# Three float32r passes for two of the second layer's seven products, with the split of their operands a step ahead

## The chip, the cores and the metric

The kernel runs on one core of one Trainium2 chip. The metric is device time of one execution, in microseconds (us), lower is better; times shown are medians of runs.

## The reference

A Fourier mixing of 8 batches of 3008 x 256 numbers (the real part of a two-dimensional transform over sequence and features) is followed by a two-layer network on the 24064 rows:

```
X = fft(x, axis=1); X = fft(X, axis=2); x = X.real.reshape(24064, 256)
h = x @ w_in                       # 256 -> 2048
g = h * clip(h + 3, 0, 6) / 6      # hard swish
out = g @ w_out                    # 2048 -> 256
```

## The kernel before

The transform is done in three parts. Stage one (`fold`, `stage1`) adds mirrored inputs on GpSimd (POOL) and multiplies them on TensorE (PE) by a cosine and sine table for 47 of the 3008 = 47 x 64 points; its result `z` goes to DRAM and comes back turned as `g`. Stage two (`stage2`) multiplies by the tables of the 64 points and leaves a chunk of 256 columns in one PSUM bank, which is copied into `q`. The transform over the 256 features is folded into `w_in` at the start, so that the first layer takes `q` directly.

The work is cut into four pairs of batches with 12 chunks each, 48 chunks in all, and every chunk into eight steps (`fc`), each for 256 of the 2048 hidden units. The last chunk of each pair has 192 columns in the second layer.

**First layer.** From chunk 3 on its products are exact splits into float32r: `split_q` splits `q` into `KQ` (high, low and rest), `split_w` has done so with the weights (`KW`), and three passes (`passes`, order rest, high, low) replace a float32 product. The work is arranged in units of 512 columns (`Unit`), mostly *joint*: the same weights for two neighbouring chunks. A unit is made up of a seed in PSUM (`seed`, ScalarE, ACT), three even passes, a copy of that sum (`keep_even`, ACT, into `s`), three odd passes into the same bank (`odd_half`), a relu of it (ACT), the value for the mirrored output `v = u - 2 s` (`other_sign`, VectorE, DVE), its relu (ACT), and two gates on DVE that write the hidden values into a slot of `A`.

**Second layer.** A 2 x 2 block product by seven products instead of eight (the weights `G` hold seven blocks, 0 = B11, 1 = B21 and so on). Products 0, 1 and 2 take `A` as it is; products 3 to 6 take sums of its blocks, which POOL makes one step ahead (`combine`, tile `c`). The seven products of a step accumulate over the eight steps in four banks (`acc`), in float32. `close`, `finish`, `store` and `turn` join the seven results at a chunk's end (`e`), transpose them on DVE into `o` and send `o` in eight DMAs of 32 KB for each half.

**Order of the work.** The schedule is written out by hand: each engine runs its instructions in the order in which the program issues them. From step 22 on, one turn of the main loop (a *cycle*) issues the odd half of one unit, the even half of the next and a share of the product stream. `place` says how many products a cycle takes (6 to 8), `due` by when a unit must be gated. `Feed` lets POOL do `fold` work when its estimated backlog allows. PSUM has four banks for `acc`, two for units (`a0`, `a1`) and two others (`y0`, `y1`): `v` lives in `y0`; stage two takes `y1`; stage one takes both. The order within one cycle before the change is: seed of the next unit; odd passes and relu; one product; stage one, where there is a piece; other sign and its relu; one product; even passes and copy `s`; the two gates; transposes; stage two, where there is one; the other products; closing and sums.

Buffers: four `x` tiles, two `z`, two `o`, two `s`, one `q` kept to the end.

Of the kernel before, what the change touches and what calls it, by code (L numbers as in the profile page):

```python
# [60 lines left out]
def kernel(  # L61
# [38 lines left out]
    xpool = ctx.enter_context(tc.tile_pool(name="xpool", bufs=4))  # L100
    ypool = ctx.enter_context(tc.tile_pool(name="ypool", bufs=1))
    zpool = ctx.enter_context(tc.tile_pool(name="zpool", bufs=2))
# [25 lines left out]
    NSLOT, CHUNK1 = 9, 3  # L128
    SPLIT = CHUNK1 * NF - 2
# [12 lines left out]
    G = consts.tile([P, 7, NF, P], F32, name="G")  # L142
# [15 lines left out]
    def x_tile(pool=xpool, tag="x", bufs=None):  # L158
        return pool.tile([P, XC, D], F32, tag=tag, bufs=bufs, name="xt")
# [8 lines left out]
    def load_forward(pr, c):  # L168
        xt = x_tile()
# [14 lines left out]
    def load_partners(pr, c):  # L184
        xr = x_tile()
        pr.xr[c] = xr
        i = pr.p * NXC + c
        gather(xr, IX[:, i:i + 1])
# [14 lines left out]
    def take_half(hb, m, pool=xpool, tag="x"):  # L203
        hb.x[m], hb.xr[m] = x_tile(pool, tag), x_tile(pool, tag)
# [167 lines left out]
    def evict_first(hb, m, ps, pt):  # L372
        k = FIRST.index(m)
        pool, tag = ((zpool, "z"), (zpool, "z"), (wpool, "z"), (wpool, "z"))[k]
        z = pool.tile([P, 2, 2, D + 1], F32, tag=tag, bufs=2, name="z")
# [100 lines left out]
    Q = []  # L476

    def q_tile(pr, gr):
        if pr.p == gr == 0:
            pr.q[0] = early.tile([P, 2, 2 * TB], F32, tag="q", name="q")  # L480
            return
        if not Q:
            Q.append(qpool.tile([P, 2, 2 * TB], F32, tag="q", name="q"))
        pr.q[gr] = Q[0]

    def stage2_half(hb, gr, copy=nc.scalar.copy, ps=None, tab=None):

        vg, i = hb.b * NSG // 2 + gr // 2, gr % 2
        if i == 0:
            q_tile(first, vg)  # L490
# [16 lines left out]
        copy(first.q[vg][:, :, i * TB:(i + 1) * TB], ps)  # L507

    def spread_part(pr, n, cols):

        i = n % 2 * TB
        qd = dpool.tile([1, TB], F32, tag="qd", name="qd")
        nc.sync.dma_start(out=qd[:, 0:cols], in_=pr.q[n // 2][P - 1:P, 1, i:i + cols])
# [13 lines left out]
    def stage2(pr, gr, i, copy=nc.scalar.copy):  # L527

        if i == 0:
            q_tile(pr, gr)  # L530
# [12 lines left out]
        copy(pr.q[gr][:, :, i * TB:i * TB + n], ps[:, :, 0:n])  # L543

# [6 lines left out]
    class Chunk:  # L551
# [3 lines left out]
        def __init__(self, pr, ck):  # L555
# [8 lines left out]
            self.n_all = pr.p * NCK + ck  # L564
            k1 = [(ck * KK + j // 2 + 1) % NK1 for j in range(KC)]
# [28 lines left out]
    def activate(ch, fc, u, v, between=None):  # L594
        nq, qn = ch.nq, QN[:, ch.n_all % 4]
        s = spool.tile([P, 2, TB], F32, tag="s", name="s")
# [6 lines left out]
        pool, tag, bufs = (early, "a", 3) if ch.n_all * NF + fc < SPLIT else (zpool, "z", 2)  # L603
# [14 lines left out]
    def split_q(ch):  # L618

        of, nq, q = ch.ck % 2 * TB, ch.nq, ch.pr.q[ch.ck // 2]  # L620
        high, low, rest = (KQ[:, j, :, ch.n_all % 3, 0:nq] for j in range(3))
        yield from split(high, low, rest, q[:, :, of:of + nq])

    def split(high, low, rest, x):
        nc.scalar.mul(high, x, 1.0 - EPS / 2.0)  # L625
        h = high.bitcast(F32)
        nc.gpsimd.tensor_tensor(low, x, h, op=AL.subtract)  # L627
        yield OPERATION
        nc.scalar.mul(rest, h, EPS)  # L629
        nc.gpsimd.tensor_tensor(rest, rest, low, op=AL.subtract)  # L630
        yield OPERATION
# [74 lines left out]
    def keep_even(un):  # L706
        un.s = spool.tile([P, 2, TB], F32, tag="s", name="s")
        nc.scalar.copy(un.wide(un.s[:]), un.wide(un.u[:]))  # L708
# [20 lines left out]
    def gates(un, m):  # L729

        h, t = (un.u, un.v)[m], un.t[:, m]
        wide = [k for k, (ch, _) in enumerate(un.parts) if not ch.last]
# [43 lines left out]
    def mlp2_first(ch, fc, halves=(0, 1)):  # L776
        a = ch.a[fc]
        for h in halves:
            if fc == 0:
                ch.acc[h] = ps_a.tile([P, 2, TB], F32, tag="acc", name="acc")  # L780
            for f in range(2):
                nc.tensor.matmul(ch.acc[h][:], G[:, (B11, B12, B21, B22)[2 * f + h], fc, :], a[:, :, f],  # L782
# [7 lines left out]

    def mlp2(ch, fc, lo, hi):
# [3 lines left out]
        order = list(enumerate(moving))  # L795
        if ch.final and fc == NF - 1:

            order[5:] = order[:4:-1]
# [4 lines left out]
        for i, mv in order[lo:hi]:  # L803

            if fc == 0 and i % 2 == 0:
                ch.acc[i // 2] = ps_a.tile([P, 2, TB], F32, tag="acc", name="acc")
            nc.tensor.matmul(ch.acc[i // 2][:, i % 2, 0:ch.n], G[:, i, fc, :], mv,  # L807
                             start=(fc == 0 and i % 2 == 0), stop=(fc == NF - 1), skip_group_check=True)
            if fc == NF - 1 and (i % 2 == 1 or i == 6):
                if i == 1:  # L810
                    ch.e = epool.tile([P, 7, TB], F32, tag="e", bufs=1, name="e")
                k = 2 * (i // 2)
                if ch.final:
                    if k == 0:
                        nc.scalar.mul(ch.e[:, 0, 0:ch.n], ch.acc[0][:, 0, 0:ch.n], 1.0 / WS)
                    continue
                if i == 6:
                    closing.append([ch, 0])
# [3 lines left out]
    def close_to(end):  # L822
        while closing and closing[0][1] < end:
            close(*closing[0])
            closing[0][1] += 1
            if closing[0][1] == 4:
                closing.pop()

    def close(ch, part):
# [10 lines left out]
        elif part == 2:  # L840
            nc.scalar.mul(e[:, 2:4], ch.acc[1][:, :, 0:ch.n], 1.0 / WS)
        else:
            plus(e[:, 5], 5, e[:, 0], -1.0)
# [11 lines left out]
    def finish_final(ch):  # L855
# [4 lines left out]
        os = [epool.tile([P, TB // DH, 2, DH], F32, tag="o", name="o") for m in range(2)]  # L860
# [19 lines left out]
    def store(ch, m, h):  # L880
        if h == 0:
            ch.o = epool.tile([P, TB // DH, 2, DH], F32, tag="o", name="o")
# [41 lines left out]
    def load_w(j, queue=nc.gpsimd, clear=None):  # L924
        kind, n, i = PIECES[j]

        pool, tag, bufs = (wpool, "st", 2) if j in STRAIGHT else (wpool, "st2", 2) if j in (2, 3) else (xpool, "x", None)
# [720 lines left out]
```

## Time and profile before

| | |
|---|---|
| median of 3 runs | 1814.73 us (1814.1 to 1815.53) |
| the profiled execution | 1814.22 us, span 1812.5 us |
| PE, DVE, ACT, POOL busy | 99%, 57%, 59%, 78% of the span |
| instructions on PE | 9024 matmuls, 9024 weight loads |
| moved by DMA | 110 MB, 61 GB/s in the mean |
| granted clock of TensorE | 0.999 in the mean |

How to read it: an engine's busy time is the union of its instructions' spans, and spans of neighbours overlap where the engine works in a pipeline; a float32 matmul stands as two records, a float32r one as one. In a timeline row the first number is the start (us from the span's start), the second the length, then the engine, line, operation, tiles (out<-in), shape and count; square brackets give the idle time before it and what ended it. In a row of groups the numbers behind the bar are the group's busy time (us), the mean duration of one (ns) and the idle time ahead of them.

### The profile page before, as it was taken

Reading aid. Unit: us, or ns where it says so; the run is one execution under the profiler, and the core shown is the slowest. Engines: PE = TensorE matmul, PEld = TensorE weight load, DVE = VectorE, ACT = ScalarE, POOL = GpSimd, SP = SyncE. Lnnn points to the kernel's source line nnn. Section 1 sums busy time; section 2 is a strip of 40 time slices with the busy share of each in tenths; the row PEclk is TensorE's granted clock in tenths of the full one; section 3 lists DMA queues with packets and bytes.
Section 4 is the critical chain, followed back from the end, with each engine's and each line's share of the span. In section 5 each row is a group of like instructions: output and inputs, shape, how many; then the busy total and the mean of one; then the engine's idle time right before and its main releaser. Section 6 shows DMA issues by size and latency. Waiting matters only on the chain.

```text
span 1812.5 us, 26823 instructions
## 1 busy us (share of the span) xinstructions
PE 1801.4 (99%) x9024; PEld 1532.6 (85%) x9024; DVE 1037.8 (57%) x2026; ACT 1077.5 (59%) x1886; POOL 1406.4 (78%) x1550
## 2 busy tenths in 40 slices
PE   9999999999999999999999999999999999999998
PEld 6688888888988888888898888888889888888887
DVE  8987555555555555555555555555555555555555
ACT  6556666665666555565566555565556556555652
POOL 5687998867778999677778899877677777777774
PEclk9999999999999999999999999999999999999999
DMA  8434342211123422121022232210111111102001
GB/s 276 117 96 122 90 107 76 51 29 40 41 64 78 107 73 60 28 45 38 19 57 69 73 101 76 63 39 16 43 32 32 41 21 41 39 21 45 17 12 33
DMA packets 160521, 110.18 MB, mean 61 GB/s; under 512 B 122292, under 2 KB 141074, under 8 KB 160382
## 3 DMA queue, kind: packets, MB, share of 16 engines
q1 hardware_dynamic: 151630, 82.22, 19.0%
q0 software_dynamic: 7504, 25.65, 4.5%
q8 instruction: 71, 1.16, 0.3%
q10 hardware_dynamic: 1248, 0.59, 0.1%
q14 instruction: 68, 0.56, 0.1%
HBM read 71.93 MB, written 36.79 MB: 60 GB/s over the span
## 4 chain that ended last, share of the span: by engine, by line
PE 96%; DVE 2%; ACT 1%; DMA 1%; issue 0%; POOL 0%; ACTq 0%; DVEq 0%; POOLq 0%
PE acc L807 61%; PE u L685 27%; PE ps L540 2%; PE ps L302 1%; PE v L590 1%; PE u L590 1%; PE acc L782 1%; ACT PM L943 0%; DMA xt<-in_x_dram,IT 0%; PE ps L504 0%; ACT t L755 0%; DMA QN<-in_x_dram 0%; DVE top L970 0%; DVE s L599 0%; DVE a L758 0%
## 5 line engine op out<-in xcount | busy, mean ns | idle before, releaser
L685 PE MATMUL u<-KQ,KW 128*128 128x512 f32 (+6 forms) x2448 | 747.6, 420 | 0.0
L807 PE MATMUL acc<-c,G 128*128 128x256 f32 (+1 forms) x3008 | 709.5, 375 | 0.1
L807 PEld LDWEIGHTS acc<-c,G 128*128 128x128 f32 x3008 | 562.2, 190 | 77.3 <-POOL c L772 4.0
L772 POOL TENSOR_TENSOR c<-A 128x512 f32<-128x512 f32 (+1 forms) x357 | 448.4, 1256 | 214.7 <-PE acc L807 211.0
L718 DVE SCALAR_TENSOR_TENSOR v<-s,u 128x512 f32<-128x512 f32 (+1 forms) x360 | 247.2, 687 | 613.0 <-ACT t L755 612.9
L807 PE MATMUL acc<-A,G 128*128 128x256 f32 (+1 forms) x2160 | 573.6, 375 | 0.0
L755 ACT ACTIVATE t<-u,half 128x512 f32<-128x512 f32 (+2 forms) x384 | 261.2, 680 | 396.1 <-PE u L685 337.8
L685 PEld LDWEIGHTS u<-KQ,KW 128*128 128x128 f32 (+1 forms) x2448 | 435.2, 190 | 62.3
L807 PEld LDWEIGHTS acc<-A,G 128*128 128x128 f32 x2160 | 396.1, 189 | 79.0 <-issue 15.9
L755 ACT ACTIVATE t<-v,half 128x512 f32<-128x512 f32 (+2 forms) x384 | 261.2, 680 | 269.6 <-DVE v L718 269.6
L758 DVE SCALAR_TENSOR_TENSOR A<-t,v 128x512 f32<-128x512 f32 (+3 forms) x478 | 250.8, 545 | 53.5 <-ACT t L755 50.5
L772 POOL TENSOR_TENSOR c<-c,A 128x256 f32<-128x256 f32 (+1 forms) x357 | 257.8, 722 | 28.0
L772 POOL TENSOR_TENSOR c<-A,c 128x256 f32<-128x256 f32 (+1 forms) x357 | 256.3, 718 | 28.0
L758 DVE SCALAR_TENSOR_TENSOR A<-t,u 128x512 f32<-128x512 f32 (+3 forms) x478 | 248.0, 539 | 0.0
L700 ACT ACTIVATE u<-QN,WN 128x512 f32<-128x512 f32 (+1 forms) x312 | 217.9, 699 | 0.0
L708 ACT COPY s<-u 128x512 f32<-128x512 f32 (+1 forms) x360 | 205.1, 570 | 0.0
L772 POOL TENSOR_TENSOR e<-e 128x256 f32<-128x256 f32 (+1 forms) x92 | 90.9, 988 | 0.1
L889 DVE STREAM_TRANSPOSE o<-e 128x256 f32<-128x256 f32 (+1 forms) x192 | 82.8, 432 | 2.7 <-POOL e L772 2.4
L627 POOL TENSOR_TENSOR KQ<-q,KQ 128x512 fp32r<-128x512 f32 (+1 forms) x45 | 56.5, 1256 | 31.4 <-ACT KQ L625 31.4
L630 POOL TENSOR_TENSOR KQ<-KQ 128x512 fp32r<-128x512 f32 (+1 forms) x45 | 56.5, 1255 | 24.9 <-ACT KQ L629 24.6
L834 DVE SCALAR_TENSOR_TENSOR e<-acc,e 128x256 f32<-128x256 f32 (+1 forms) x184 | 69.9, 416 | 6.7 <-PE acc L807 1.9
L313 DVE COPY z<-ps 112x512 f32<-112x512 f32 x24 | 16.6, 691 | 66.4 <-PE ps L302 56.6
(147 smaller groups left out, 1070.8 us busy)
## 6 DMA issues: line engine op xcount, KB each, us to landing
out_dram<-o SPq DMA_DIRECT2D x744, 32.0 KB
T<-in_c_stage_dram SPq DMA_DIRECT2D x26, 512.0 KB
g<-zd SPq DMA_DIRECT2D x42, 256.0 KB
zd<-z SPq DMA_DIRECT2D x48, 192.0 KB
QN<-qd SPq DMA_DIRECT2D x43, 128.0 KB
xt<-in_x_dram SPq DMA_DIRECT2D x21, 256.0 KB
st<-in_moe_w_out_dram POOLq DMA_DIRECT2D x7, 512.0 KB, 5.6
xt<-in_x_dram SPq DMA_DIRECT2D x17, 192.0 KB
```

Of the source, the lines that this page charges most:

```text
L627: nc.gpsimd.tensor_tensor(low, x, h, op=AL.subtract)
L630: nc.gpsimd.tensor_tensor(rest, rest, low, op=AL.subtract)
L685: nc.tensor.matmul(un.wide(un.u[:]) if un.joint else un.u[:, i, 0:un.nq], un.weights(j, blk, i, rows), un.moving(j, blk, rows), start=Fals ...
L700: nc.scalar.activation(un.wide(un.u[:]), un.wide(row), AF.Identity, scale=WN[:, f:f + 1])
L708: nc.scalar.copy(un.wide(un.s[:]), un.wide(un.u[:]))
L718: nc.vector.scalar_tensor_tensor(v, s, -2.0, u, op0=AL.mult, op1=AL.add)
L755: nc.scalar.activation(t, h, AF.Relu, bias=half[:], scale=scale)
L758: nc.vector.scalar_tensor_tensor(dst, t, 1.0, h, op0=AL.min, op1=AL.mult)
L772: (eng or nc.gpsimd).tensor_tensor(out, in0, in1, op=AL.add)
L807: nc.tensor.matmul(ch.acc[i // 2][:, i % 2, 0:ch.n], G[:, i, fc, :], mv, start=(fc == 0 and i % 2 == 0), stop=(fc == NF - 1), skip_group_c ...
L834: nc.vector.scalar_tensor_tensor(o, acc(i), sign / WS, x, op0=AL.mult, op1=AL.add)
L889: nc.vector.transpose(o[:, 0:n // DH, h], ch.r[m, h][:, 0:n].rearrange("p (j i) -> p j i", i=DH))
```

## The change

From chunk 8 on (`CHUNK2`), products 0 and 1 (`NFR = 2`) are done by three float32r passes each, into the same bank: first the high part times the high weight, later the rest and the low part. The order of a step becomes: both high passes, product 2, product 3, the other four passes, products 4, 5, 6. The weights of these two blocks live in tiles of their own (`GH`) and are split during chunk 7 (`split_weights`, into `GH` and `GK`).

The hidden values are split by `split_gates` a step ahead: an ACT scaling into float32r, issued right behind the first group of the step; an ACT copy of it into a PSUM bank and two DVE operations (low and rest), issued at the end of the cycle. They go into one tile `J`, written for step s+1 while step s still runs.

`q` is no longer copied: `split_q` scales straight from the bank on ACT, copies 32 rows of it on ACT for the row that is spread, and makes low and rest on DVE from the bank; its two POOL operations and the DVE copy go.

In the cycle, the seed is issued at the end of the cycle before, for the unit after next; stage one's products stand behind the fifth group of the step instead of behind the first product; closing is cut into five parts; at a chunk's end `keep_even` is done by DVE between the gates. From chunk 8 on each cycle has seven products, also at the borders of the pairs.

Buffers: one tile each for the two kinds of `x` (the next forward piece is loaded when a piece is folded, the partners a little sooner), one `z`, one `o` and one `s`; the transposes into `o` move from steps 2, 3, 4, 5 of a chunk to 2, 3, 5, 6.

```diff
+    CHUNK2, NFR = 8, 2
...
-    G = consts.tile([P, 7, NF, P], F32, name="G")
+    G = consts.tile([P, 7 - NFR, NF, P], F32, name="G")
+    GH = [consts.tile([P, NFR, P], F32, tag=f"GH{fc}", name="GH") for fc in range(NF)]
...
-    def split_q(ch):
-        of, nq, q = ch.ck % 2 * TB, ch.nq, ch.pr.q[ch.ck // 2]
-        high, low, rest = (KQ[:, j, :, ch.n_all % 3, 0:nq] for j in range(3))
-        yield from split(high, low, rest, q[:, :, of:of + nq])
-    def split(high, low, rest, x):
+    def split_q(ch, ps):
+        x = ps[:, :, 0:ch.nq]
+        high, low, rest = (KQ[:, j, :, ch.n_all % 3, 0:ch.nq] for j in range(3))
+        ch.row = qpool.tile([P, TB], F32, tag="row", name="row")
         nc.scalar.mul(high, x, 1.0 - EPS / 2.0)
-        h = high.bitcast(F32)
-        nc.gpsimd.tensor_tensor(low, x, h, op=AL.subtract)
-        yield OPERATION
-        nc.scalar.mul(rest, h, EPS)
-        nc.gpsimd.tensor_tensor(rest, rest, low, op=AL.subtract)
-        yield OPERATION
+        nc.scalar.copy(ch.row[P - DH:P, 0:ch.nq], ps[P - DH:P, 1, 0:ch.nq])
+        def others():
+            nc.vector.scalar_tensor_tensor(low, x, 1.0, high.bitcast(F32), op0=AL.mult, op1=AL.subtract)
+            nc.vector.scalar_tensor_tensor(rest, high.bitcast(F32), 1.0 + EPS, x, op0=AL.mult, op1=AL.subtract)
+        split_later.append(others)
...
+    HIGH, OTHERS = (0,), (2, 1)
+        high, others = ([(i, j) for i in range(NFR)] for j in (HIGH, OTHERS))
+        rest = [[(i, None)] for i in range(NFR, 7)]
+        order = [high] + rest[:2] + [others] + rest[2:]
...
+            for j in parts or (None,):
+                w = weight(i, fc) if not j else GK[:, j - 1, fc, i]
+                nc.tensor.matmul(o, w, moving[i] if j is None else parts_tile(ch, fc)[:, j, i, 0:ch.n],
+                                 start=(fc == 0 and i % 2 == 0 and j in (None, 0)), stop=(fc == NF - 1),
+                                 skip_group_check=True)
...
+    def split_gates(ch, fc):
+        a = ch.a[fc].rearrange("p m f n -> p (m f) n")[:, 0:NFR, 0:ch.n]
+        high, low, rest = (parts_tile(ch, fc)[:, j, :, 0:ch.n] for j in range(3))
+        nc.scalar.mul(high, a, 1.0 - EPS / 2.0)
+        yield
+        ps = ps_u.tile([P, 2, TB], F32, tag="y0" if split_later or lent[0] else "y1", name="high")[:, 0:NFR, 0:ch.n]
+        nc.scalar.copy(ps, high.bitcast(F32))
+        nc.vector.scalar_tensor_tensor(low, ps, -1.0, a, op0=AL.mult, op1=AL.add)
+        nc.vector.scalar_tensor_tensor(rest, ps, 1.0 + EPS, a, op0=AL.mult, op1=AL.subtract)
+        yield
...
-        if nx:
-            seed(nx)
         if un:
             odd_half(un)
...
         products(1)
-        for gen in parts:
-            next(gen)
+        flush(high_of)
         if un:
             other_sign(un)
...
-        products(size - 2)
-        close_to(3)
+        products(size - 4)
+        for gen in parts:
+            next(gen)
+        products(2)
+        close_to(4)
+        if others_at < 5:
+            flush(others_of)
+        split_rest()
+        if cycle + 2 < len(units):
+            seed(units[cycle + 2])
```

More of the change, by code (lines that the diff above doesn't have):

```diff
@@ L789, in mlp2_first, with order_of @@
                     nc.scalar.mul(ch.r[m, h], ch.acc[h][:, m], (1 - 2 * m) / WS)
+    HIGH, OTHERS = (0,), (2, 1)
+    def order_of(ch, fc):
+        end = ch.final and fc == NF - 1
+        if not ch.split:
+            return [[(i, None)] for i in range(7)]
+        high, others = ([(i, j) for i in range(NFR)] for j in (HIGH, OTHERS))
+        rest = [[(i, None)] for i in range(NFR, 7)]
+        if end:
+            rest[-2:] = rest[:-3:-1]
+        order = [high] + rest[:2] + [others] + rest[2:]
+        while len(order) > 7:
+            order[0:2] = [order[0] + order[1]]
+        return order
     def mlp2(ch, fc, lo, hi):
@@ L802, in mlp2 @@
                 freed.append(ch.slot.pop(fc))
[L803 to L818, printed above, removed]
+            if fc == NF - 1 and not ch.final:
+                closing.append([ch, 0])
@@ L1440, in sums @@
             cost += FINISH[fc - 1]
-        for gen in splits.get(s, ()):
-            next(gen)
-            cost += OPERATION
-        feed.cycle(cost, (4.75 if s < SPLIT else 4.33) + 0.9 * (s in middle_fns) + 2.05 * (s in behind))
+        feed.cycle(cost, (4.75 if s < SPLIT else 4.25) + 0.9 * (s in middle_fns) + 2.05 * (s in behind))
     def turns_out(s):
@@ L1500 @@
         un, nx = (units[i] if i < len(units) else None for i in (cycle, cycle + 1))
-        turn_of[0] = cycle + 1
+        turn_of[0], start = cycle + 1, done
         size = place[cycle + 1] - place[cycle]
```

254 lines of the change are left out of this document (175 added, 79 removed).

## The prediction

> **What bounds the kernel now.** I read the busy shares and the chain of the page first, then one chunk by windows, then the timeline of TensorE, and last the queues of the two engines that take on work.
>
> ```profile
> PE 1801.4 (99%) x9024; PEld 1532.6 (85%) x9024; DVE 1037.8 (57%) x2026; ACT 1077.5 (59%) x1886; POOL 1406.4 (78%) x1550
> ...
> PE 96%; DVE 2%; ACT 1%; DMA 1%; issue 0%; POOL 0%; ACTq 0%; DVEq 0%; POOLq 0%
> ```
>
> TensorE is busy 99% of the span and is 96% of the chain that ended last: every nanosecond taken off its queue comes off the end, as long as nobody makes it wait. A chunk of the steady part, eight steps, shows the same:
>
> ```profile
> 1499.40:1535.65 36.25, 36.25 (x170) 31.17 (x169) 19.31 (x34) 21.34 (x36) 26.31 (x29) 1.00 0.16 32
> ```
>
> 36.25 us, so 4.53 us a step, all of it PE at full granted clock, with DVE (third pair of numbers) at 53% and ACT at 59%.
>
> What a product costs cannot be read from the mean duration of a group, since matmuls overlap in the pipeline; it is the distance between starts. One cycle (a unit of the first layer woven into one step of the second), TensorE alone:
>
> ```profile
> 1502.89 1.05 PE L685 MATMUL u<-KQ,KW 127*128 127x512 f32 x3
> 1503.78 1.03 PE L807 MATMUL acc<-A,G 128*128 128x256 f32 x4
> 1504.46 1.04 PE L685 MATMUL u<-KQ,KW 128*128 128x512 f32 x3
> 1505.34 0.59 PE L807 MATMUL acc<-A,G 128*128 128x256 f32 x2
> 1505.77 1.89 PE L807 MATMUL acc<-c,G 128*128 128x256 f32 x8
> 1507.31 0.82 PE L685 MATMUL u<-KQ,KW 127*128 127x512 f32 x2
> ```
>
> A float32 product of 256 columns is two records (14 for a step's seven products), and two records last from 1505.34 to 1505.77: 0.43 us a product. The cycle is 1507.31 - 1502.89 = 4.42 us. Of 1503.78 to 1505.34 = 1.56, four records are 0.86, so the three float32r passes over 512 columns take 0.70.
>
> The change needs passes over 256 columns. Such groups exist, where a unit is not joint:
>
> ```profile
> 528.83 1.03 PE L807 MATMUL acc<-c,G 128*128 128x256 f32 x4
> 529.50 1.06 PE L685 MATMUL u<-KQ,KW 128*128 128x256 f32 x6
> 530.41 0.81 PE L807 MATMUL acc<-c,G 128*128 128x256 f32 x3
> ```
>
> 530.41 - 528.83 = 1.58, less four records (0.86): six passes, each with a weight load of its own, take 0.72, or 0.12 each.
>
> **TensorE's part.** From chunk 8 on the first two products of a step become three passes each: 0.86 us of float32 goes, 6 x 0.12 = 0.72 comes. That is 0.14 us less a step. 40 chunks of 8 steps are touched; the last chunk of each of the four pairs has 192 columns, where float32 scales to 0.32 a product and three passes lie between 0.27 (scaled) and 0.36 (not below 0.12 each). I take nothing there; the ends are a gain of 3 us and a loss of 3 over these 32 steps (64 products by 0.05 or 0.04). The other 288 steps give 288 x 0.14 = 40.3 us.
>
> One page would price this otherwise. The Trainium skill, "TensorE: Matmul & The Clock Gate", section "Back-to-back issue gap", has a warm matmul cost its columns over 2.4 GHz plus 2.5 ns, which is 109 ns for 256. The trace disagrees with its 120 ns; by the page the saving would be 0.20 a step, 59 us in all, as an estimate.
>
> **ACT and DVE, which take on the splitting.** A step gets on ACT a scaling into float32r (two products at once, 512 wide) and a copy of it into a PSUM bank, on DVE two operations that make the low and the remaining part. Nearest rows:
>
> ```profile
> L629 ACT ACTIVATE KQ<-KQ 128x512 fp32r<-128x512 f32 x41 | 26.2, 640 | 0.0
> L625 ACT ACTIVATE KQ<-q 128x512 fp32r<-128x512 f32 x41 | 26.2, 639 | 0.0
> ...
> L837 ACT ACTIVATE e<-acc 128x256 f32<-128x256 f32 x43 | 17.0, 396 | 0.0
> ...
> L640 ACT ACTIVATE high<-KW 128x512 f32<-128x512 f32 x8 | 4.8, 602 | 0.3
> ```
>
> ```profile
> L834 DVE SCALAR_TENSOR_TENSOR e<-acc,e 128x256 f32<-128x256 f32 x172 | 66.1, 420 | 6.6 <-PE acc L807 1.9 <-ACT e L837 0.8
> L543 DVE COPY q<-ps 128x512 f32<-128x512 f32 x36 | 23.6, 655 | 0.0
> ...
> L643 DVE SCALAR_TENSOR_TENSOR KW<-W,high 128x512 fp32r<-128x512 f32 x8 | 5.4, 679 | 0.0
> ```
>
> So 0.64 + 0.60 on ACT and 2 x 0.68 on DVE. Whether that hides is a matter of where it lies in the cycle. The two queues of the cycle shown above:
>
> ```profile
> 1503.98 0.69 ACT L755 ACTIVATE t<-u,half 128x512 f32<-128x512 f32 x1 [0.69 <-PE u L685]
> 1505.43 0.69 ACT L755 ACTIVATE t<-v,half 128x512 f32<-128x512 f32 x1 [0.76 <-DVE v L718]
> 1506.02 0.58 ACT L708 COPY s<-u 128x512 f32<-128x512 f32 x1
> 1506.48 0.71 ACT L700 ACTIVATE u<-QN,WN 128x512 f32<-128x512 f32 x1
> ```
>
> ```profile
> 1504.70 0.69 DVE L718 SCALAR_TENSOR_TENSOR v<-s,u 128x512 f32<-128x512 f32 x1 [2.29 <-ACT t L755]
> 1505.31 0.68 DVE L758 SCALAR_TENSOR_TENSOR A<-t,u 128x512 f32<-128x512 f32 x1
> 1506.15 0.69 DVE L758 SCALAR_TENSOR_TENSOR A<-t,v 128x512 f32<-128x512 f32 x1 [0.16 <-ACT t L755]
> ```
>
> Count from the start of the odd passes, 1503.78 - 0.70 = 1503.08. Before: first relu 0.90, v 1.62, gate 2.23, second relu 2.35, copy s 2.94 to 3.52, second gate 3.07 to 3.76. After, with a cycle of 4.42 - 0.14 = 4.28:
>
> The scaling for step s+1 is issued between the two relus, and the gap of 0.76 there holds its 0.64: nothing moves. The copy into PSUM follows copy s (starts overlap, 1506.48 - 1506.02 = 0.46 apart): 3.40 to 4.00. DVE's two operations follow it, 0.61 apart as 1504.70 and 1505.31 are: 4.00 to 5.30, which is 1.02 of the next cycle. The next v comes at 1.62, and TensorE reads these parts only after the odd passes, the high passes, a product, the even passes and another product: 0.70 + 0.24 + 0.43 + 0.70 + 0.43 = 2.50. The seed that now ends ACT's cycle runs 3.9 to 4.6, or 0.32 of the next, and is needed at 1.37. Copy s must be done before the next odd passes: 3.52 against 4.28. The margins are 0.6 (DVE), 1.0 (seed), 0.76 (copy s). A cost of zero, covered by those; uncovered, each 0.6 on either queue would be 0.6 on PE.
>
> Once per chunk more is queued. The split of q loses its two POOL operations and DVE's copy (0.66) and gets two DVE operations (1.36), one ACT scaling fewer and a copy of 32 rows more. It waits for stage two:
>
> ```profile
> 1485.88 1.04 PE L685 MATMUL u<-KQ,KW 128*128 128x512 f32 x3
> 1486.77 1.05 PE L540 MATMUL ps<-T,g 128*128 128x128 f32 x8
> 1487.65 0.60 PE L807 MATMUL acc<-A,G 128*128 128x256 f32 x2
> ```
>
> That cycle is 1487.65 - 1486.77 = 0.88 longer. With q's scaling (0.64) and row copy (0.40, as L837 over the same 256 columns) ahead, the copy into PSUM ends at 5.0, DVE's four operations at 7.4, 2.2 of the next cycle: v is 0.6 late, copy s ends at 4.1 instead of 3.52, still before 4.28. At a chunk's end copy s goes to DVE (0.66), and four closing operations of 0.42 fall in two cycles: v 0.1 to 0.2 late, free. DVE's load per step is 5 x 0.61 plus an eighth of (4 closings of 0.42, 4 transposes of 0.44, 1.36, 0.66), 3.73 of 4.53 - 0.14 = 4.39: 85%, against 53%. Behind a late DVE operation stand v, both gates and then TensorE.
>
> **Where a wait is added.** Stage one writes two banks, one of them v's. Its PE work is moved from behind the first product to behind the fifth group:
>
> ```profile
> 616.90 0.59 PE L807 MATMUL acc<-A,G 128*128 128x256 f32 x2
> 617.43 1.09 PE L302 MATMUL ps<-y,F 47*64 47x512 f32 x8
> 618.45 0.70 PE L807 MATMUL acc<-A,G 128*128 128x256 f32 x2
> ```
>
> ```profile
> L302 PE MATMUL ps<-y,F x192: 376/590/641, 180.9 to 1170.9; 47*64 47x512 f32 x180, 47*64 47x256 f32 x12
> ```
>
> TensorE would arrive there at 2.50 + 0.48 + 0.43 = 3.41 of the cycle, but v is read until the second gate ends at 3.76; with the hand-over 0.4 us of waiting, and with it everything behind on PE's queue. 192 records in groups of 8 are 24 pieces: +9.6 us. If the gate were done in time it is 0; behind a gate 0.6 late it is 24 us.
>
> **Buffers.** One o buffer: the second half's transposes, two cycles after the first half's, wait for its eight stores.
>
> ```profile
> L894 SPq DMA_DIRECT2D out_dram<-o x740: 536/536/3873, 120.2 to 1800.9; - x185
> L889 DVE STREAM_TRANSPOSE o<-e x192: 370/437/446, 114.7 to 1807.8; 128x256 f32<-128x256 f32 x176, 128x192 f32<-128x192 f32 x16
> L900 SPq DMA_DIRECT2D out_dram<-o x8: 316/429/439, 1806.1 to 1809.6; - x8
> ```
>
> The transposes end at about 4.1, eight issues of 0.54 end at 8.4. The last store of all begins at 1809.6 and the span ends at 1812.5, so landing is at most 2.9 after an issue begins: 10.8. The second half transposes at 2 x 4.28 + 3.7 = 12.2. No wait, with 1.4 to spare; only in chunk 1, where the halves are one step apart, up to 2 us once, which I book. The x tiles hold one piece instead of two: POOL may wait for a load two cycles after it is asked for, but it loses q's two operations per chunk, and its sums are a step ahead. Taken as 0; not traced, so up to +5 in the range. In the 192-column chunks a cycle is 5 x 0.32 + 6 x 0.12 + 2 x 0.65 to 0.72, about 3.6 to 3.8, just above the 3.52 at which copy s ends: 0.1 of waiting on 24 steps, +2.4.
>
> Sum against the profiled execution, 1814.2 (its span is 1812.5, the median of the runs 1814.7): 1814.2 - 40.3 + 9.6 + 2 + 2.4 = 1788. The half microsecond between it and the median is left aside.
>
> **The rivals.** (a) Stage one's bank is free in time, because nothing else in the cycle is late and the gate is early: 1788 - 9.6 = 1778. Against it: 3.41 and 3.76 come from rows. (b) A short pass costs a quarter of the float32 product, 0.43 / 4 = 0.1075, because nothing but the streaming of columns counts: 0.86 - 6 x 0.1075 = 0.215 a step, 288 x 0.215 = 62 us, 1766. Against it: the six passes of the rows take 0.12 each. (The page named above stands close to this case.) (c) DVE becomes the bound. With every operation at its full duration instead of overlapped starts, its cycle is 3 x 0.69 + 2 x 0.68 + 0.68 (the eighth of the extras) = 4.1; if its waits for ACT (0.16 for the second relu, some 0.3 for the copy into PSUM) stay, 4.6. Then the cycle is 4.6, over the 4.53 of now: 320 x 0.07 = +22, 1836. It decides from 0.14 us of lateness per step that does not recover. For it: five DVE operations in a ring with ACT, where each sixth waits. Against it: starts 0.61 apart, and 0.6 of slack before v. (d) Waits of the late kind (q's split, stores, stage one) add up to 20 to 40 us: 1808 to 1828, about where it was.
>
> **The numbers.** Forecast 1788 with its neighbours up to 1806: 0.55. (a) 0.17, (b) 0.06, (d) 0.08, (c) 0.14. Faster: 0.55 + 0.17 + 0.06 and a quarter of (d), 0.80; same 0.05; slower (c) and a little of (d), 0.15. What can be told from no change is about 0.2%, 3.6 us. The likeliest case's own range is 1779 to 1806; with (a), (b) and half of (d), 1766 to 1814.
>
> **What would show it.** Right: a plain cycle of 4.28 in the TensorE timeline, six short passes 0.12 apart at line 807's successor, PE idle of about 0.4 before each of the 24 stage-one groups released by DVE, DVE near 80% and ACT near 80% busy, POOL lower. Wrong: PE idle in every cycle, waiting for ACT's copy s or DVE's rest; v starting later than 1.7 in plain cycles; passes at other than 0.12; idle behind POOL's sums or a store.

## The result and the profile after

The changed kernel takes 1820.73 us (median of 9 runs, 1819.12 to 1821.6) against 1814.73 before (9 runs, 1814.07 to 1816.91). The ratio is 1.003, with a 95% interval of 1.0019 to 1.004: slower by 6 us, where 1788 was forecast. The profiled execution took 1819.84 us, its span is 1818.1, both 5.6 more than before.

In the changed kernel line 841 is the second layer's matmul (before: 807), 702 the first layer's (685), 317 stage one's (302), 792 POOL's sums (772), 778 the gates (758), 735 the value `v` (718), 862 and 867 ACT's scaling and copy for the split of the gates, 868 and 869 DVE's two operations of it, 639 and 640 the split of `q`, 878 to 885 that of the weights, 901 the closing on DVE, 271 POOL's sum of a piece of `x`.

The page of the changed kernel, busy shares and the chain that ended last, by engine and by line:

```profile
PE 1783.8 (98%) x9664; PEld 1524.8 (84%) x9664; DVE 1472.0 (81%) x2789; ACT 1382.1 (76%) x2496; POOL 1305.3 (72%) x1468
...
PE 85%; DVE 5%; DMA 3%; ACT 2%; POOL 2%; issue 1%; SPq 1%; ACTq 0%; DVEq 0%; POOLq 0%
PE acc L841 52%; PE u L702 24%; DMA xt<-in_x_dram 2%; PE ps L551 2%; PE ps L317 2%; PE acc L802 1%; POOL c L792 1%; PE v L601 1%; ACT t L775 1%; PE u L601 1%; DVE v L735 1%; SPq L963 1%; PE spare L1081 0%; DVE J L868 0%; DVE J L869 0%
```

PE's busy time fell by 17.6 us and the span grew by 5.6: PE is now idle where before it was not. Its share of the chain is 85% instead of 96%, and a transfer is in the chain, the load of `xt`.

The steady part did what was forecast. The chunk that answers to the 36.25 us of before, by windows, and one plain cycle, TensorE alone:

```profile
1511.72:1546.76 35.04, 35.04 (x185) 30.80 (x184) 29.95 (x52) 29.08 (x52) 23.98 (x27) 1.00 0.14 34
```

```profile
1519.38 1.05 PE L702 MATMUL u<-KQ,KW 127*128 127x512 f32 x3
1520.27 0.40 PE L841 MATMUL acc<-J,GH 128*128 128x256 f32 x2
1520.51 0.60 PE L841 MATMUL acc<-A,G 128*128 128x256 f32 x2
1520.75 1.05 PE L702 MATMUL u<-KQ,KW 128*128 128x512 f32 x3
1521.64 0.59 PE L841 MATMUL acc<-c,G 128*128 128x256 f32 x2
1521.88 0.82 PE L841 MATMUL acc<-J,GK 128*128 128x256 f32 x4
1522.54 1.46 PE L841 MATMUL acc<-c,G 128*128 128x256 f32 x6
1523.65 0.58 PE L702 MATMUL u<-KQ,KW 127*128 127x512 f32 x1
```

PE is busy all of the 35.04 us, 1.21 less than before, with DVE now at 85%. The cycle is 1523.65 - 1519.38 = 4.27 (forecast 4.28). From 1521.64 to 1522.54 lie a product of 0.43 and four short passes: 0.47, so 0.118 each (forecast 0.12). The 109 ns that the prediction worked out from the Trainium skill, "TensorE: Matmul & The Clock Gate", section "Back-to-back issue gap", was too low here; the formula there is the gap of an isolated matmul, which the prediction did not say.

DVE and ACT in the same cycle:

```profile
1521.19 0.70 DVE L735 SCALAR_TENSOR_TENSOR v<-s,u 128x512 f32<-128x512 f32 x1 [0.56 <-ACT t L775]
1521.79 0.68 DVE L778 SCALAR_TENSOR_TENSOR A<-t,u 128x512 f32<-128x512 f32 x1
1522.64 0.69 DVE L778 SCALAR_TENSOR_TENSOR A<-t,v 128x512 f32<-128x512 f32 x1 [0.17 <-ACT t L775]
```

Counted from the start of the odd passes, 1520.27 - 0.70 = 1519.57, `v` begins at 1.62 and the second gate ends at 3.76, both as worked out in the prediction. So the question is where the rest went. The waits of the changed kernel (total us, times, longest):

```profile
POOL xt L271 <- DMA xt<-in_x_dram: 49.2, 13, 9.4
...
PEld acc L841 <- POOL c L792: 22.2, 17, 4.3
...
PE acc L841 <- POOL c L792: 11.3, 6, 3.8
```

POOL waits for the load of a piece of `x`, up to 9.4 us, and PE and its weight loads wait for POOL's sums `c`. In the trace of before this wait of POOL does not appear (one of 4.4 us for a load of `x` at the start stands in both), nor does PE's for `c`; the weight loads waited 4.0 us for it there.

The time by place, from the trace. A step is taken from the start of its first product group to that of the next step's:

```
                                        predicted   measured (us)
36.25 -> 35.0 a chunk, 288 steps          -40.3      -44  (288 x 0.153)
loads of x late, last pair                  0        +16
24 pieces of stage one                     +9.6      +14.6
start of the splits, chunks 7 and 8         0        about +7
chunks of 192 columns and the one behind   +2.4      +4.2
first steps of chunks 10, 22, 34            0        +3.4
last chunk (47), to its last product        0        +2.6
chunk 1, one o buffer                      +2        +2.0
sum                                       -26        about +6
```

The span grew by 5.6; what is left out here (the end behind the last product, 0.6 longer, and some tenths elsewhere) is below 1 us.

### The profile page after: what moved, and what is told of

It is laid out like the page before. It is cut to its first block, busy times and chain, and to the rows that moved or that the text cites. A ratio compares the mean times of both kernels' runs of the same rounds, so it can differ in the third digit from the quotient of the medians.

```text
span 1818.1 us, 29912 instructions
## 1 busy us (share of the span) xinstructions
PE 1783.8 (98%) x9664; PEld 1524.8 (84%) x9664; DVE 1472.0 (81%) x2789; ACT 1382.1 (76%) x2496; POOL 1305.3 (72%) x1468
## 4 chain that ended last, share of the span: by engine, by line
PE 85%; DVE 5%; DMA 3%; ACT 2%; POOL 2%; issue 1%; SPq 1%; ACTq 0%; DVEq 0%; POOLq 0%
PE acc L841 52%; PE u L702 24%; DMA xt<-in_x_dram 2%; PE ps L551 2%; PE ps L317 2%; PE acc L802 1%; POOL c L792 1%; PE v L601 1%; ACT t L775 1%; PE u L601 1%; DVE v L735 1%; SPq L963 1%; PE spare L1081 0%; DVE J L868 0%; DVE J L869 0%
## 5 line engine op out<-in xcount | busy, mean ns | idle before, releaser
L841 PE MATMUL acc<-c,G 128*128 128x256 f32 (+1 forms) x3008 | 766.5, 377 | 15.3 <-POOL c L792 11.3
L841 PEld LDWEIGHTS acc<-c,G 128*128 128x128 f32 x3008 | 535.4, 190 | 101.4 <-POOL c L792 22.2
L868 DVE SCALAR_TENSOR_TENSOR J<-high,A 128x512 fp32r<-128x512 f32 (+1 forms) x315 | 212.3, 674 | 67.5 <-ACT high L867 39.8
L841 PE MATMUL acc<-J,GK 128*128 128x256 f32 (+1 forms) x1260 | 257.7, 327 | 1.9 <-DVE J L869 1.7
L841 PE MATMUL acc<-A,G 128*128 128x256 f32 (+1 forms) x720 | 211.7, 375 | 0.5 <-DVE e L901 0.5
L869 DVE SCALAR_TENSOR_TENSOR J<-high,A 128x512 fp32r<-128x512 f32 (+1 forms) x315 | 210.7, 669 | 0.0
L841 PEld LDWEIGHTS acc<-J,GK 128*128 128x128 f32 x1260 | 193.6, 190 | 18.8 <-DVE J L869 3.8
L862 ACT ACTIVATE J<-A 128x512 fp32r<-128x512 f32 (+1 forms) x315 | 193.2, 613 | 0.0
L867 ACT COPY high<-J 128x512 f32<-128x512 f32 (+1 forms) x315 | 186.0, 590 | 8.8 <-DVE KQ L869 5.7
L725 ACT COPY s<-u 128x512 f32<-128x512 f32 (+2 forms) x315 | 179.2, 569 | 0.0
L841 PEld LDWEIGHTS acc<-J,GH 128*128 128x128 f32 x630 | 117.2, 189 | 25.0
```

The costliest lines, as they stand in the source:

```text
L841: nc.tensor.matmul(o, w, moving[i] if j is None else parts_tile(ch, fc)[:, j, i, 0:ch.n], start=(fc == 0 and i % 2 == 0 and j in (None, 0) ...
L862: nc.scalar.mul(high, a, 1.0 - EPS / 2.0)
L867: nc.scalar.copy(ps, high.bitcast(F32))
L868: nc.vector.scalar_tensor_tensor(low, ps, -1.0, a, op0=AL.mult, op1=AL.add)
L869: nc.vector.scalar_tensor_tensor(rest, ps, 1.0 + EPS, a, op0=AL.mult, op1=AL.subtract)
```

## The experiments

Each ratio is against the kernel before in the experiment's own session: 1815.13 us for *x_even*, *x_47*, *stage_back* and *before_stage_fwd*, 1815.5 for *even_later*, *even_apart*, *even_c9* and *even_all*, 1814.71 for *x_46*, *even_c20* and *even_near*. A difference of medians from two sessions can be off by as much as these differ. Kernels with the load's loop have one line more, so their line numbers are one higher.

**Why the load is late.** The stall of the last pair, SP's queue first, then POOL, then PE, in the changed kernel:

```profile
988.84 3.47 SPq L963 DMA_DIRECT2D out_dram<-o  x6
992.41 1.02 SPq L194 DMA_DIRECT2D xt<-in_x_dram  x2
...
1004.59 1.26 POOL L271 TENSOR_TENSOR xt<-xt 111x508 f32<-111x508 f32 x1 [8.66 <-DMA xt<-in_x_dram]
...
1008.18 1.22 PE L841 MATMUL acc<-c,G 128*128 128x256 f32 x2 [3.13 <-POOL c L792]
```

The piece's two loads, one for each batch of the pair, are issued from 992.41 on. POOL can begin its sum only at 1004.59, 12.2 us later. It is idle from 995.93 on, 3.5 us after the issue: six stores of `o` stand ahead of the loads in SP's queue, and POOL had done with the tile at 986.61. POOL's queue is in order: the sums `c` of the second layer stand behind, and PE stops for 3.13 us. The same place twelve chunks earlier, where the pair before is folded:

```profile
560.24 1.16 SPq L194 DMA_DIRECT2D xt<-in_x_dram  x2
...
565.10 1.27 POOL L271 TENSOR_TENSOR xt<-xt 111x508 f32<-111x508 f32 x1 [1.33 <-DMA xt<-in_x_dram]
```

Here it is 4.9 us, with the same six stores ahead and POOL again idle 3.5 us after the issue. The difference is in `load_forward`: the last batch of all has no 48th row to read (`nr = N1 + 1 if i < B - 1 else N1`), and its load is 47 rows of 4 KB, 188 KB. What the DMA engines moved, in forty slices of 0.1 us, while this load was on its way:

```profile
DMA  0000100010374100100000100000010000010000
GB/s 41 0 41 0 41 41 0 41 41 1 43 45 3 41 0 41 41 0 41 41 0 41 41 0 41 0 41 41 0 41 41 0 41 41 0 41 0 41 41 0
```

This is 999 to 1003 us. 41 GB/s in a slice of 0.1 us is one packet of 4 KB; there are 25 of them in 4 us, one behind the other, 0.16 us apart, and the busy share of the sixteen engines shows 0 or 1 tenth, but for three slices in which small packets pass too: one engine is at work on this load. 47 rows at that pace are 7.5 us. The Trainium skill, "DMA: Bandwidth & Descriptors", section "Why a DMA increments its semaphore by 16 and not by 1", gives a rule for this: a transfer is dealt to the largest number of engines, up to 16, that divides the slowest dimension (of a size other than 1) of both its sides. Here that is the rows: 47 is a prime, so one; 48 gives 16. Three runs test it.

*x_even: the 47 rows cut in two.*

```diff
-            rows, o = x_pn[i * N1:i * N1 + nr], xt[b * PB:b * PB + nr]
-            nc.sync.dma_start(out=o[:, 0:n, :], in_=rows[:, c * XC + 1:c * XC + 1 + n, :])
+            for r0, r1 in ((0, 32), (32, nr)) if nr == N1 else ((0, nr),):
+                rows, o = x_pn[i * N1 + r0:i * N1 + r1], xt[b * PB + r0:b * PB + r1]
+                nc.sync.dma_start(out=o[:, 0:n, :], in_=rows[:, c * XC + 1:c * XC + 1 + n, :])
...
```

> The changed kernel with the load of the last batch's 47 rows cut into 32 and 15 rows. Theory (the 47-row load lands some 8 us later than the 48-row loads of the other batches, POOL waits for it with only one piece of x in hand, the sums are late and TensorE waits): chunks 25 to 30 lose their stalls of 4.8, 5.7, 2.3, 1.5 us, some 16 us in all, 1804 us; POOL's wait for the forward x load falls from 49 us to under 12. Rival (one piece of x is too little however it is loaded, since the store DMAs stand ahead of the load on SP's queue): the same stalls, within 3 us of 1820.

Measured: 1807.09 us (1806.09 to 1807.87), ratio 0.9953 (0.9936 to 0.997), 13.6 us less than the changed kernel. The wait of POOL (expected under 12), and the sum of the piece shown above:

```profile
POOL xt L272 <- DMA xt<-in_x_dram: 14.8, 9, 2.4
```

```profile
1000.47 1.28 POOL L272 TENSOR_TENSOR xt<-xt 111x508 f32<-111x508 f32 x1 [1.12 <-DMA xt<-in_x_dram]
```

The three issues begin at 995.83, so the piece is there within 4.6 us. From chunk 2 on the two traces agree within 0.1 us a chunk outside chunks 25 to 30, where 16.1 us are gone (chunk 25: 5.3, chunk 28: 6.0). The 16 us of the ledger are these. Ahead of chunk 2 this profiled execution lost 3.4 us: the first product of chunk 1 began 1.7 us later (94.97 for 93.27), and chunk 1 took 1.7 us more (47.32 for 45.58). Both vary between the profiled executions of kernels that are the same program up to there (93.3 to 95.8, and 45.6 to 47.3), so single gains of 2 us in the medians are to be read with the steps beside them. The median is 3 us above the 1804 expected. The rival, that the stores ahead of the load are enough for the stalls, is out; but they cost the load its lead, and no run moved them.

*x_46: the same load cut behind row 46.* Two engines by the rule, instead of one.

```diff
-            for r0, r1 in ((0, 32), (32, nr)) if nr == N1 else ((0, nr),):
+            for r0, r1 in ((0, 46), (46, nr)) if nr == N1 else ((0, nr),):
```

> The load of the last batch is cut behind row 46 (46 rows and 1) instead of behind row 32. Theory (the rows of one load are dealt to as many DMA engines, 16 at most, as divide their number evenly: all for 48 and 32, 15 for 15, two for 46, one for 47): two engines take 23 rows of 4 KB each, 0.165 us apart, 3.8 us in place of 47 x 0.165 = 7.8; the load lands some 7 us after its issue, where 47 rows took 11 and 48 rows 4. The sums of a piece are then late by under 2 us where they were late by 5: of the 16 us lost in the last pair 2 to 5 stay, 1809 to 1812 us. Rival 1 (any load that is not 48 or 32 rows is slow, or the number of bytes decides): 46 rows take as long as 47, 1819 to 1822. Rival 2 (any cut helps, because the two parts run side by side): as with the cut at 32, 1807.

Measured: 1808.44 us (1807.13 to 1809.86), ratio 0.9964 (0.995 to 0.9978). Issue and sum:

```profile
993.29 1.35 SPq L195 DMA_DIRECT2D xt<-in_x_dram  x3
...
1001.48 1.26 POOL L272 TENSOR_TENSOR xt<-xt 111x508 f32<-111x508 f32 x1 [4.66 <-DMA xt<-in_x_dram]
```

8.2 us from the first issue to the sum, between 12.2 (47 rows) and 4.6 (cut at 32): two engines with 23 rows each save 24 packets of 0.16 us, 3.8 us, and 4.0 were measured. Of the 16.1 us lost in chunks 25 to 30, 3.5 stay. The theory's size (2 to 5) holds and rival 1 falls; the median is just below the theory's range. The medians alone would not separate it from rival 2 (1807); the wait of 4.66 beside 1.12 does.

*x_47: 47 rows for every second batch*, so that all pairs have the slow load.

```diff
-            nr = N1 + 1 if i < B - 1 else N1
+            nr = N1
```

> The changed kernel with 47 rows loaded for every second batch instead of 48 (the 48th is not used). Theory (47 rows are the cause): the pairs folded in chunks 13 to 18 now stall as those of chunks 25 to 30 do, +12 to +16 us there, and less in chunks 3 to 8 where a step is longer: 1832 to 1840 us. Rival (what is slow in chunks 25 to 30 is another thing, such as the place in memory or other traffic): within 3 us of 1820.

Measured: 1838.1 us (1836.45 to 1839.93), ratio 1.0121 (1.0104 to 1.0138):

```profile
POOL xt L271 <- DMA xt<-in_x_dram: 91.8, 21, 8.6
...
PE acc L841 <- POOL c L792: 20.1, 12, 3.1
```

The loss of the last pair appears in the pair one earlier too: 16.0 us in chunks 13 to 18 (5.3, 1.1, 4.0, 5.3 and 0.4), and 1.5 in chunk 5. So the cause of the largest item is shown from both sides.

**Stage one.** Two pieces of the changed kernel, a plain one and one in the step behind a stage two, PE's weight loads and DVE:

```profile
567.93 0.69 DVE L778 SCALAR_TENSOR_TENSOR A<-t,v 128x512 f32<-128x512 f32 x1 [0.17 <-ACT t L775]
```

```profile
568.36 0.52 PEld L317 LDWEIGHTS ps<-y,F 47*64 47x64 f32 x8 [0.33 <-issue]
```

```profile
589.59 0.68 DVE L639 SCALAR_TENSOR_TENSOR KQ<-ps,KQ 128x512 fp32r<-128x512 f32 x1
590.19 0.68 DVE L640 SCALAR_TENSOR_TENSOR KQ<-KQ,ps 128x512 fp32r<-128x512 f32 x1
590.78 0.69 DVE L735 SCALAR_TENSOR_TENSOR v<-s,u 128x512 f32<-128x512 f32 x1
...
592.23 0.69 DVE L778 SCALAR_TENSOR_TENSOR A<-t,v 128x512 f32<-128x512 f32 x1 [0.17 <-ACT t L775]
```

```profile
592.10 0.19 PEld L317 LDWEIGHTS ps<-y,F 47*64 47x64 f32 x2 [0.33 <-issue]
592.97 0.20 PEld L317 LDWEIGHTS ps<-y,F 47*64 47x64 f32 x6 [0.68 <-DVE A L778]
```

In the plain piece the gate ends at 568.62, and the step is 5.80 us: 1.53 above the plain 4.27, where before it was 5.63 - 4.42 = 1.21. In the second piece DVE first does the split of `q`, two operations ahead of `v`; `v` begins at 2.2 of its cycle instead of 1.62, the gate ends at 592.92 and the weight loads wait until 592.97. That step is 6.34, 2.07 above plain. Eight of the sixteen pieces of pairs 2 and 3 lie so. Four runs moved stage one.

*stage_back: back behind the first group.*

```diff
         products(1)
+        for gen in parts:
+            next(gen)
         flush(high_of)
...
-        products(size - 4)
-        for gen in parts:
-            next(gen)
-        products(2)
+        products(size - 2)
```

> The changed kernel with stage one's products back behind the first group of the step. Theory (they wait for the second gate to leave v's bank): the 24 pieces cost 1.11 us each again instead of 1.78 in the mean, -14.6 us less what the later v brings, 1806 to 1810 us. Rival (with DVE and ACT at 80% the wait only moves: v comes later, copy s and TensorE's odd passes wait): within 4 us of 1820.

Measured: 1820.72 us (1818.75 to 1822.23), ratio 1.0028 (1.0018 to 1.0038): no gain. Plain pieces are 0.2 cheaper (5.60), those behind a stage two 0.5 dearer (6.85), for there the piece now waits for the bank of stage two, until the split of `q` from it is done:

```profile
PE ps L317 <- DVE KQ L640: 10.3, 8, 1.3
```

Eight times, as many as there are such pieces. The rival was right that the wait only moves.

*before_stage_fwd: the kernel before, with stage one at the changed kernel's place.*

```diff
-        for gen in parts:
-            next(gen)
         if un:
             other_sign(un)
...
-        products(size - 2)
+        products(size - 4)
+        for gen in parts:
+            next(gen)
+        products(2)
```

> The kernel before with one part of the change alone: stage one's products behind the fifth product of the step instead of the first. Theory (the wait for v's bank belongs to the place, not to the load on DVE): arrival 0.70 + 0.43 + 0.43 + 0.70 + 3 x 0.43 = 3.55 against a gate that ends at 3.76, so 0.2 to 0.3 us a piece in plain cycles and up to 0.7 where a cycle has six products, +6 to +11 us, 1821 to 1826. Rival (only the loaded DVE makes the gate late): within 2 us of 1814.7.

Measured: 1829.57 us (1829.16 to 1829.7), ratio 1.0077 (1.006 to 1.0094): 14.4 us more, above the 6 to 11 expected. A plain piece costs only 0.17 more; the rest lies at chunk borders (steps of 7.35, 5.33, 6.11). So the later place costs time without the splits too, but not through every piece.

*even_later: x_even with stage one one product later, before the last.*

```diff
-        products(size - 4)
+        products(size - 3)
         for gen in parts:
             next(gen)
-        products(2)
+        products(1)
```

> The 47-row load cut in two as in x_even, and stage one's products one float32 product later, between products 5 and 6. Theory (only the second gate holds them up): arrival 3.41 + 0.43 = 3.84 after the start of the odd passes against a gate at 3.76 to 3.80, so the plain pieces lose their 0.31 and those behind stage two half of their 0.85; 1807.1 - 8 = 1799 us. Rival (the copies of z, then as much later on ACT and DVE, push the split of the next step behind TensorE's need): 1805 to 1810 us, with TensorE waiting for DVE's rest in the step after a piece.

Measured: 1804.58 us (1803.42 to 1805.01), ratio 0.9937 (0.992 to 0.9953), 2.5 less than x_even. The gain lies in chunks 3 to 7 alone (0.43 to 0.61 each). In pairs 2 and 3 the plain piece is 0.3 cheaper and the step behind it as much dearer (5.49 and 4.64 instead of 5.80 and 4.27). The rival was mostly right: the wait is handed on to the next seed.

*even_apart: x_even, and from pair 2 on no piece in the step behind a stage two.*

```diff
-... and s not in middle_fns and s not in behind:
+... and s not in middle_fns and (s < NCK * NF or s - 1 not in middle_fns) and s not in behind:
```

> x_even with no stage-one piece in the step behind a stage two, from the second pair on. Theory (q's split makes v 0.6 late in that step, so the piece waits 0.85 instead of 0.31): 8 or 9 pieces get 0.5 us each back, and the step after them 0.15; 1802 to 1803 us. Rival (the piece costs what it costs wherever it stands): 1807 us.

Measured: 1800.49 us (1800.25 to 1800.65), ratio 0.9916 (0.9899 to 0.9932), 6.6 less than x_even. By the steps from chunk 2 on 5.6 us are gained, 2.8 in each of the two pairs, about what the theory counted (8 or 9 times 0.5, and 0.15 in the step behind); that the median is below the 1802 to 1803 expected lies ahead of chunk 2. The steps of 6.34 are gone, the pieces are 5.80 all but the last of a pair. The weight loads' wait for the gate, x_even first, then even_apart:

```profile
PEld ps L318 <- DVE A L779: 9.2, 14, 1.2
```

```profile
PEld ps L318 <- DVE A L779: 3.7, 6, 1.2
```

So the dear part of stage one was its neighbourhood with the split of `q`, which the prediction had priced but not counted.

**The start of the splits.** The end of chunk 7 and start of chunk 8 in the changed kernel, DVE and PE:

```profile
379.91 0.42 DVE L879 TENSOR_SCALAR high<-GK 128x256 f32<-128x256 f32 x1
380.37 0.42 DVE L880 SCALAR_TENSOR_TENSOR GK<-GH,high 128x256 fp32r<-128x256 f32 x1
380.82 0.42 DVE L882 TENSOR_SCALAR GH<-high 128x256 fp32r<-128x256 f32 x1
381.16 0.42 DVE L883 SCALAR_TENSOR_TENSOR high<-high,GK 128x256 f32<-128x256 f32 x1
381.49 0.75 DVE L901 SCALAR_TENSOR_TENSOR e<-acc,e 128x256 f32<-128x256 f32 x2
383.10 0.69 DVE L868 SCALAR_TENSOR_TENSOR J<-high,A 128x512 fp32r<-128x512 f32 x1 [0.86 <-ACT high L867]
```

```profile
381.96 0.70 PE L841 MATMUL acc<-A,G 128*128 128x256 f32 x2 [0.55 <-DVE e L901]
...
384.44 0.74 PE L841 MATMUL acc<-J,GK 128*128 128x256 f32 x4 [0.65 <-DVE J L869]
```

Four operations for the weights, 1.6 us, and the closing of chunk 7 stand ahead of the split of the gates, which PE then waits for. The 0.86 us in front of the split is a wait for ACT's copy, and ACT's queue shows the same operations behind it:

```profile
381.62 0.38 ACT L885 ACTIVATE GK<-high 128x256 fp32r<-128x256 f32 x1 [1.04 <-DVE high L883]
381.90 0.68 ACT L775 ACTIVATE t<-u,half 128x512 f32<-128x512 f32 x1
382.47 0.60 ACT L867 COPY high<-J 128x512 f32<-128x512 f32 x1
```

ACT stands 1.04 us until DVE's four are done, then finishes the weights, and comes to the copy only behind a relu. The weights are also not all split during chunk 7: steps with a stage one or a stage two are passed over, and three of the eight sets fall into steps 64, 65 and 67. Chunk 8 takes 41.9 us, where a plain chunk takes 35.0 and one with a piece of stage one 36.7 (chunk 15).

*even_c9: x_even with the start at chunk 9* (`CHUNK2, NFR = 9, 2`).

> x_even with the float32r passes starting in chunk 9, the weights split in chunk 8. Theory (chunk 8 lost some 7 us because the weights' four DVE operations of 0.42 a step stood between the gates and the split that TensorE waits for): chunk 8 gives up its 1.2 us of gain and gets back 4 to 6; 1802 to 1804 us. Rival (chunk 8 is slow for the stage-one pieces of the first pair and the first splits, wherever the weights are split): the loss moves to chunk 9, 1807 to 1809 us.

Measured: 1804.44 us (1803.79 to 1806.11), ratio 0.994 (0.9923 to 0.9956). Chunks 7 and 8 gain 3.1 and 3.5, chunk 9 loses 6.2: the loss moves along with the start, as the rival said. The median lies just above the theory's 1802 to 1804, but not by its gain: by the steps only 0.5 us is gained, and the rest against x_even lies ahead of chunk 2, where the times vary as said above.

*even_c20: x_even with the start at chunk 20* (`CHUNK2, NFR = 20, 2`).

> With the last batch's load cut at 32, and the passes from chunk 20 on, where the weights are split in chunk 19, in which no piece of stage one lies. With the start at chunk 8, chunks 8 to 19 took 2.8 us more than before, 7 of it at the start of the splits. Here chunks 8 to 18 go back to float32 (about -2.8 against the kernel with the cut, and +2 to +3 for the later place of stage one in six pieces). Theory (the start costs what it does because the weights' four VectorE operations a cycle stand ahead of the first splits of the gates): 4 to 7 us are lost in chunks 19 and 20, 1811 to 1815 us in all. Rival (the start costs because pieces of stage one lie in the same steps and push the weights' splits back): chunks 19 and 20 lose 1.5 us at most, 1806 to 1809 us.

Measured: 1810.59 us (1809.52 to 1811.42), ratio 0.9974 (0.9964 to 0.9984). No piece of stage one lies near, and chunk 20 is still 4.6 us above plain (steps of 7.16, 5.00, 5.22), chunk 19 1.6 above its float32 cycle: 6.2 us, within the theory's 4 to 7, though the median is just below its range. A piece in the way is not needed for the loss. DVE's order is the same as above, and PE waits more:

```profile
825.50 0.70 PE L842 MATMUL acc<-A,G 128*128 128x256 f32 x2 [1.26 <-DVE e L902]
```

What belongs to the weights' operations and what to the closing can be told in part. Steps 155 to 157, 161 and 162 each follow on a set of the weights' operations, with no closing; they hold 3.3 of the 6.2 us. The other 2.9 are step 160, where the closing and the first splits come on top; the same closing one chunk on, without weights, costs nothing (step 168: 4.27). Within step 160 the parts are not told apart.

**The mends together.** *even_all*: x_even, even_later, even_c9 and even_apart in one, and the second half of the first chunk's transposes one step later, so that the first half's stores are out of the single `o` buffer:

```diff
-            elif prev and 3 <= fc < 7:
-                store(prev, (fc - 3) // 2, 1 - fc % 2)
+            elif prev and fc in (3, 4, 6, 7):
+                store(prev, fc // 6, (fc - 3) % 3)
```

> The three edits together with x_even, and the first chunk's second half of the output one step later, so that its transposes do not wait for the stores of the first. If the causes add up: 1807 - 8 (later) - 4 (weights) - 3 (apart, with less left to gain behind later) - 2 (first chunk) = 1790 us. If DVE's queue is what all of them share, less than half of that: 1798 to 1802 us.

Measured: 1794.84 us (1794.33 to 1796.25), ratio 0.9887 (0.987 to 0.9903): 1.1% faster than the kernel before, the best of all. The single gains in the medians lead from the changed kernel to 1820.7 - 13.6 - 2.5 - 2.65 - 6.6 = 1795.4, before the store's 2 us (step 14 of chunk 1: 4.75 instead of 6.99); but these medians hold what varies ahead of chunk 2. By the steps from chunk 2 on the single gains are 16.2, 1.8, 0.5 and 5.6, 24.1 together, and all four at once gain 23.8: they add. The 1790 of the expectation rested on single gains that had been expected larger.

*even_near*: even_all with the start back at chunk 8, and no piece of stage one begun there:

```diff
-    CHUNK2, NFR = 9, 2
+    CHUNK2, NFR = 8, 2
...
-... and s not in behind:
+... and not 63 <= s < 67 and s not in behind:
```

> The four mends together, but with the passes from chunk 8 on and no piece of stage one begun in steps 63 to 66. Theory (the weights' VectorE operations cost the start): no better than with the start at chunk 9, 1794 to 1797 us. Rival (the piece of stage one in step 66 costs it): chunk 8 loses 3 us less than the 6 it lost, and one more chunk gains its 1.2, 1791 to 1793 us.

Measured: 1795.84 us (1795.11 to 1796.26), ratio 0.9893 (0.9876 to 0.9909): as even_all, and within the theory's range. The piece is gone from step 66 (5.22 instead of 7.35), but it has only moved to step 67, which takes 7.05 instead of 4.27; chunk 8 takes 42.0 as in x_even (41.9). So this run does not part theory and rival; even_c20, with no piece near, does.

## Why the prediction was wrong

**Right.** What a pass costs (0.118 for 0.12), the saving of a step (0.153 for 0.14), the inner times of the plain cycle (`v` at 1.62, second gate until 3.76, DVE's two operations 4.04 to 5.33 of the cycle for 4.00 to 5.30), DVE and ACT near 80% (81 and 76), POOL lower (72 for 78), and 2 us for the one `o` buffer in chunk 1 (2.0 in the changed kernel's profile, 3.7 in x_even's). Rivals (b) and (c) are out with these: no plain cycle is held up by DVE.

**The step that failed: "Taken as 0; not traced, so up to +5".** The x tiles' term measured 16 us. Its reasoning gave a load two cycles, 8.5 us, and looked at POOL's own work. Two things differed: SP's queue, with six stores ahead, left 3.5 us between issue and need, and the load took 12.2. With 48 rows the same 3.5 us cost POOL 1.3 us of waiting; the length of the load is what made the loss. The prediction did not ask for that length, and the trace of before had it. What was moved there from 1010 to 1026 us, in forty slices of 0.4 us, around a load issued at 1010.54:

```profile
DMA  3333596600000122100000122100013223210001
GB/s 72 72 72 72 111 169 256 195 0 20 20 31 31 40 72 68 45 20 31 20 31 31 44 72 70 40 20 21 18 23 72 56 53 70 59 38 12 0 0 41
...
xt<-in_x_dram SPq DMA_DIRECT2D x1, 188.0 KB
```

After a burst at 256 GB/s, in which the other batch's load goes, 20 to 31 GB/s trickle on until about 1021, 10 us after the issue. With four tiles POOL never waited for it; with one for these pieces it does (the number of tiles was not varied by itself). This alone, 13.6 us in the medians, turns a gain into the loss that was seen.

**Stage one, 9.6: 14.6.** The mechanism was right, the size off. The prediction itself says that behind a gate 0.6 late all pieces would cost 24 us, and that `v` is 0.6 late in the cycle behind a stage two; it did not count how many pieces stand in just that cycle. Eight do.

**Missing terms.** The start of the splits (about 7 us) was not in the sum at all: the prediction weighed the steady state and a chunk's end, not the steps in which the weights are split as well. The last chunk (2.6), in which steps of 2.3 us leave less room for the splits, and the first steps of chunks 10, 22 and 34 (3.4), where the closing falls behind a stage two, are read from step times and were not tested.

Rival (d), late waits of 20 to 40 us beyond the sum, 1808 to 1828, has the measured time and about the measured amount: some 50 us of waits, of which the sum had 14, against 44 saved. But it named the split of `q`, the stores and stage one; the largest item, the load, was not among them, so that its hit is luck in part. It had 0.08 because the prediction priced the one wait that it could see and left the others to a rival, instead of asking of each buffer taken away what its transfer takes.

## What to carry to other kernels

When buffers are taken away, read from the trace of before how long each of their transfers takes from issue to landing, the odd-sized one too, and what stands ahead of it in its queue: a slow one is invisible as long as there are tiles enough. Cut the rows of a load so that many engines share it (32 and 15, not 47). And when a change adds work to an engine with a given order, price it at the busiest places, where it starts and where two events of a chunk fall into neighbouring steps, not in the plain cycle alone.

## What was not expected of the hardware

One row less made a load two to three times as long: 47 rows of 4 KB reached POOL some 12.2 us after the first issue, one packet each 0.16 us; cut at 46 rows it was 8.2, cut at 32 it was 4.6, and 48 rows took 4.9. The Trainium skill's rule named above fits all four.
